# Four stacked attention layers, run one after the other or as one stream of steps on one core

## Chip, cores, metric

One core of one Trainium2 chip. The metric is the device time of one launch in microseconds (us), median of several runs. Each kernel was timed next to the kernel before on the same chip.

## What has to be computed

The reference is four layers, A, B, A, B, over 2048 tokens of width 640, each with a layer norm before it and a residual around it. Both A layers share one set of weights, and so do both B layers. Cut to what matters:

```python
def A(x):                          # 32 heads of 192; 64 segments of 32 tokens
    mem = mem0                     # 8 rows
    for s in range(64):
        h = concatenate([mem, x[segment s]])          # 40 tokens
        q, k, v = h @ Wq, h @ Wk, h @ Wv              # each 640 x 6144
        p = softmax(where(mask, q @ k.T * scale, -1e9))
        o = (p @ v) @ Wo                              # 6144 x 640
        mem = o[:8]                # the next segment needs it
        outs.append(o[8:])

def B(x):                          # 32 heads of 20; each token sees itself and
    ...                            # the tokens 2, 4, ... 14 before it

x = x + A(ln(x)); x = x + B(ln(x)); x = x + A(ln(x)); x = x + B(ln(x))
```

The loop over segments is a true recurrence, so the segments of one layer cannot be batched. And B looks back 14 tokens at most, so it needs only the present and the previous segment.

The weights of A are 4 x 640 x 6144 values in bf16, 31.5 MB. Neither kernel keeps all of them on the chip: part stays resident there, and the rest is streamed again, in the kernel before for every segment.

## The kernel before

It runs the layers one after the other; the activations between them lie in DRAM. In an A layer the 32 units of weights (960 KB each) are 20 resident and 12 streamed per segment, in a ring of four buffers, from a copy in DRAM that is laid out for long contiguous pieces.

```python
# projections: 40 tokens (in a slot of 64 columns) stationary, 384 weight columns moving,
# two heads-pairs side by side in the array
def stream_group(st_cur, wt):
    for c in range(NCH):
        for j2 in range(2):
            nc.tensor.matmul(ps[SLOT * j2:SLOT * (j2 + 1), :], lhsT=st_cur[:, c, :],
                             rhs=wt[:, j2, c * UW:(c + 1) * UW], ...,
                             tile_position=(0, SLOT * j2))
# (cut)
for i in range(16 + 2):                       # 8 units of K, 8 of Q
    if i < 16:
        ps = stream_group(st_cur, get_pair(i))
        nc.scalar.copy(out=stage[:, :], in_=ps[:, :])
    if 1 <= i <= 16:
        do_transposes(i - 1)                  # 6 on TensorE: keys and queries come out
                                              # token-major and must be turned
    if 10 <= i:
        do_scores(i - 2)
# (cut) softmax with mask, max, subtract, Exp, sum, reciprocal, multiply; transposes of P;
#       V and P.V; output projection with 320 moving columns; then the tail of the segment:
nc.scalar.copy(out=part_sb[rs, 0:320], in_=w_ps[0][rs, :])
nc.vector.tensor_copy(out=part_sb[rs, 320:640], in_=w_ps[1][rs, :])
for c in range(NCH):
    nc.tensor.matmul(m_ps[:, c, :], lhsT=part_sb[:, c * P:(c + 1) * P], rhs=selm_r[:, :], ...)
nc.vector.tensor_copy(out=st_nxt[:, :, 0:NM], in_=m_ps[:, :, :])      # next memory
```

A B layer works on four blocks of 512 tokens, with elementwise products for the eight offsets and matmuls with 0/1 matrices that sum over a head.

Of the kernel before, what the change touches and what calls it, by code (L numbers as in the profile page):

```python
# [11 lines left out]
F32 = mybir.dt.float32  # L13
F32R = mybir.dt.float32r
ACT = mybir.ActivationFunctionType
ALU = mybir.AluOpType
AX = mybir.AxisListType
PSUM = bass.MemoryType.PSUM
DRAM = bass.MemoryType.DRAM

def _knob(name, default):
    return default

# [3 lines left out]
NCH = 5  # L27
H = 32
DH = 192
HE = H * DH  # L30
NM = 8
SEG = 32
LTOK = NM + SEG
SLOT = 64
UW = 384
NU = 3 * HE // UW
NHP = 16
NWO = HE // P
EPS = 1e-5
NEG = -1.0e9  # L40

BH = 32
BDH = 20
BW = 8
BDIL = 2
BPAD = (BW - 1) * BDIL


def _ln_rows(nc, pool, x_sb, np_, out_bf, eps_t, dve_stats=False):
    st = pool.tile([P, 4], F32, name="ln_st")  # L50
    if dve_stats:
        bst = pool.tile([P, 2, nc.vector.BN_STATS_DIM], F32, name="ln_bst")
        xr = x_sb[:np_, :].rearrange("p (s f) -> p s f", s=2)
        for s_ in range(2):
            nc.vector.bn_stats(out=bst[:np_, s_, :], in_=xr[:, s_, :])
        nc.vector.bn_aggr(out=st[:np_, 0:2], in_=bst[:np_, :, :])
    else:
        junk = pool.tile([P, D], BF16, name="ln_junk")
        nc.scalar.activation(out=junk[:np_, :], in_=x_sb[:np_, :], func=ACT.Identity, accum_out=st[:np_, 0:1])  # L59
        nc.scalar.activation(out=junk[:np_, :], in_=x_sb[:np_, :], func=ACT.Square, accum_out=st[:np_, 1:2])  # L60
        nc.vector.tensor_scalar(out=st[:np_, 0:2], in0=st[:np_, 0:2], scalar1=1.0 / D, scalar2=None, op0=ALU.mult)
        nc.vector.tensor_tensor(out=st[:np_, 2:3], in0=st[:np_, 0:1], in1=st[:np_, 0:1], op=ALU.mult)
        nc.vector.tensor_tensor(out=st[:np_, 1:2], in0=st[:np_, 1:2], in1=st[:np_, 2:3], op=ALU.subtract)
    nc.scalar.activation(out=st[:np_, 1:2], in_=st[:np_, 1:2], func=ACT.Sqrt, bias=eps_t[:np_, :], scale=1.0)
    nc.vector.reciprocal(out=st[:np_, 1:2], in_=st[:np_, 1:2])
    nc.vector.scalar_tensor_tensor(out=st[:np_, 3:4], in0=st[:np_, 0:1], scalar=-1.0, in1=st[:np_, 1:2], op0=ALU.mult, op1=ALU.mult)
    nc.scalar.activation(out=out_bf[:np_, :], in_=x_sb[:np_, :], func=ACT.Identity, scale=st[:np_, 1:2], bias=st[:np_, 3:4])


NPAIR = 32  # L70
PAIRW = 2 * NCH * UW


def _pair_src(Wq, Wk, Wv, Wo, w, j2):
    if w < 24:
        Wsrc = (Wk, Wq, Wv)[w // 8].rearrange("d h e -> d (h e)")
        u = 2 * (w % 8) + j2
        return Wsrc[:, u * UW:(u + 1) * UW].rearrange("(c p) n -> p c n", p=P), NCH
    Wo2 = Wo.rearrange("h e d -> (h e) d")
    n0 = 24 * j2 + 3 * (w - 24)  # L80
    return Wo2[n0 * P:(n0 + 3) * P, :].rearrange("(m p) d -> p m d", p=P), 3


def prearrange_weights(tc, dram, Wq, Wk, Wv, Wo, pairs):
    nc = tc.nc
    Wr = dram.tile([NPAIR, P, 2, NCH * UW], BF16, name="Wr")
    engs = [nc.sync, nc.scalar, nc.gpsimd]
    cnt = 0
    for w in pairs:
        for j2 in range(2):  # L90
            src, a = _pair_src(Wq, Wk, Wv, Wo, w, j2)
            engs[cnt % 3].dma_start(out=Wr[w, :, j2, :].rearrange("p (a b) -> p a b", a=a), in_=src)
            cnt += 1
    return Wr


def a_res_pairs():
    extra = [int(x) for x in _knob("KDEV_RES_EXTRA", "6,14,22,30").split(",") if x != ""]
    return sorted([w for w in range(NPAIR) if w % 2 == 1] + extra)


def a_prologue(tc, x_in, n_seg, consts, dram, lname, pp, pps, ps_tag):
    nc = tc.nc
    ident = consts["ident"]
    eps_t = consts["eps"]
    S = n_seg * SEG
    XT = dram.tile([n_seg, P, NCH * SEG], BF16, name=f"XT_{lname}")
    n_tiles = (S + P - 1) // P
    for t in range(n_tiles):
        r0 = t * P  # L110
        np_ = min(P, S - r0)
        nsg = np_ // SEG
        x_sb = pp.tile([P, D], x_in.dtype, name="x_sb")
        nc.sync.dma_start(out=x_sb[:np_, :], in_=x_in[r0:r0 + np_, :])
        xn = pp.tile([P, D], BF16, name="xn")
        _ln_rows(nc, pp, x_sb, np_, xn, eps_t, dve_stats=True)
        tp = pps.tile([P, NCH, P], BF16, name="tp", tag=ps_tag)
        for c in range(NCH):
            nc.tensor.transpose(out=tp[:, c, :np_], in_=xn[:np_, c * P:(c + 1) * P], identity=ident[:np_, :np_])
        xT_sb = pp.tile([P, 4, NCH, SEG], BF16, name="xT_sb")  # L120
        nc.vector.tensor_copy(out=xT_sb[:, :nsg, :, :].rearrange("p s c t -> p c s t"),
                              in_=tp[:, :, :np_].rearrange("p c (s t) -> p c s t", t=SEG))
        nc.sync.dma_start(out=XT[4 * t:4 * t + nsg, :, :].rearrange("s p f -> p s f"),
                          in_=xT_sb[:, :nsg, :, :].rearrange("p s c t -> p s (c t)"))
    return XT


def a_layer(ctx0, tc, x_in, x_out, mem0, Wr, Worig, n_seg, consts, dram, lname, res_pairs=None, ring=4, XT=None, direct0=False):
    nc = tc.nc
    ident = consts["ident"]  # L130
    eps_t = consts["eps"]
    S = n_seg * SEG
    scale = float(DH) ** -0.5
    if res_pairs is None:
        res_pairs = a_res_pairs()
    ring = int(_knob("KDEV_RING", ring))
    res_pairs = set(res_pairs)

    with ExitStack() as ctx:
        if XT is None:  # L140
            with ExitStack() as pctx:
                pp = pctx.enter_context(tc.tile_pool(name=f"apro_{lname}", bufs=2))
                pps = pctx.enter_context(tc.tile_pool(name=f"apro_ps_{lname}", bufs=2, space=PSUM))
                XT = a_prologue(tc, x_in, n_seg, consts, dram, lname, pp, pps, "tp")

        wres = ctx.enter_context(tc.tile_pool(name=f"wres_{lname}", bufs=1))
        wring = ctx.enter_context(tc.tile_pool(name=f"wring_{lname}", bufs=ring))
        pers = ctx.enter_context(tc.tile_pool(name=f"apers_{lname}", bufs=1))
        work1 = ctx.enter_context(tc.tile_pool(name=f"awork1_{lname}", bufs=1))
        stg = ctx.enter_context(tc.tile_pool(name=f"astage_{lname}", bufs=2))  # L150
        vtp = ctx.enter_context(tc.tile_pool(name=f"avt_{lname}", bufs=3))
        psA = ctx.enter_context(tc.tile_pool(name=f"psA_{lname}", bufs=3, space=PSUM))
        psT = ctx.enter_context(tc.tile_pool(name=f"psT_{lname}", bufs=2, space=PSUM))
        psS = ctx.enter_context(tc.tile_pool(name=f"psS_{lname}", bufs=2, space=PSUM))
        psM = ctx.enter_context(tc.tile_pool(name=f"psM_{lname}", bufs=1, space=PSUM))

        res_tiles = {}
        engs = [nc.sync, nc.scalar]
        for idx, w in enumerate(sorted(res_pairs)):
            t_ = wres.tile([P, 2, NCH * UW], BF16, name=f"wp{w}")  # L160
            for j2 in range(2):
                src, a = _pair_src(*Worig, w, j2)
                engs[(2 * idx + j2) % 2].dma_start(out=t_[:, j2, :].rearrange("p (a b) -> p a b", a=a), in_=src)
            res_tiles[w] = t_
        engs = [nc.sync, nc.sync]
        dma_cnt = [0]

        direct_first = [direct0]

        def get_pair(w):  # L170
            if w in res_tiles:
                return res_tiles[w]
            t_ = wring.tile([P, 2, NCH * UW], BF16, name="wnr")
            if direct_first[0]:
                for j2 in range(2):
                    src, a = _pair_src(*Worig, w, j2)
                    nc.sync.dma_start(out=t_[:, j2, :].rearrange("p (a b) -> p a b", a=a), in_=src)
                nc.scalar.dma_start(out=Wr[w, :, :, :], in_=t_[:])
            else:
                engs[dma_cnt[0] % 2].dma_start(out=t_[:], in_=Wr[w, :, :, :])  # L180
            dma_cnt[0] += 1
            return t_

        ST0 = pers.tile([P, NCH, SLOT], BF16, name="ST0")
        nc.gpsimd.memset(ST0[:], 0.0)
        ST = [ST0, ST0]
        QTs = [pers.tile([P, 2, 3, SLOT], BF16, name=f"QT{i}") for i in range(3)]
        for i in range(3):
            nc.gpsimd.memset(QTs[i][:], 0.0)
        KT = pers.tile([P, NHP, 3, LTOK], BF16, name="KT")  # L190
# [927 lines left out]
```

## Time and profile before

| | kernel before |
|---|---|
| time, median of 4 runs | 5406.16 us (5403.37 to 5409.18) |
| start | 125 us |
| first A, first B, second A, second B | 2319, 375, 2294, 291 us |
| TensorE busy, matmuls | 90% of the span, 80,920 |
| weights moved by the streaming queue | 1557 MB |

The way to read it: first which engine is full, then in which stretches, then what that engine waits for inside a stretch. The lines for the first two are in the prediction. For the third, these are the largest waits of TensorE inside the first A layer, between 500 and 2400 us (columns: engine, tile and line that waited, for whom; total us, times, longest us):

```profile
PE m_ps L395 <- ACT part_sb L390: 42.8, 53, 0.8
PE o_ps L349 <- DVE vt L367: 13.0, 53, 0.6
...
PE qkv_ps L241 <- DMA wnr<-Wr: 1.9, 3, 0.9
```

In 1900 us, some 53 segments, TensorE waits once a segment for the copy of the output (`part_sb`) and once for the copy of V, both under a microsecond. Streamed weights cost it almost nothing, though the stream nearly fills the DMA.

### The profile page before, as it was taken

What the parts mean: (1) busy time and instruction counts of PE and PEld (TensorE: products, weight loads), DVE (VectorE), ACT (ScalarE), POOL (GpSimd) and SP (SyncE); (2) the same over time, 40 slices, a digit from 0 to 9 for tenths busy, and PEclk for the clock granted to TensorE, in tenths of its full rate; (3) what the DMA queues carried; (4) which work ended last, traced back from release to release, by engine and by line L of the source; (5) the groups of instructions that cost most, each with busy time, mean ns of one, the idle gap of its engine ahead of it and who ended that gap; (6) DMA issues with size and microseconds to landing.
All of it is one profiled execution on the core that took longest, in us unless ns stands there. A gap on an engine that the chain in (4) does not pass through costs nothing. (4 is left out here: it accounts for less than half of the span.)

```text
span 5404.5 us, 183041 instructions
## 1 busy us (share of the span) xinstructions
PE 4851.5 (90%) x80920; PEld 3395.4 (63%) x80920; DVE 2591.0 (48%) x7273; ACT 2218.3 (41%) x5244; POOL 427.2 (8%) x573
## 2 busy tenths in 40 slices
PE   2899999999999999996749999999999999999777
PEld 1666666666666666663326666666666666666533
DVE  2444444444444444445734444444444444444376
ACT  1344444434444444435524434444344434444454
POOL 0000000000000000003200000000000000000131
PEclk8999999999999999997979999999999999999889
DMA  8999999999999999980189999999999999999700
GB/s 264 356 337 330 339 338 336 335 334 336 337 337 333 336 335 339 329 315 34 35 270 334 335 335 337 338 336 332 337 338 333 336 336 336 333 337 331 267 11 15
DMA packets 329209, 1616.19 MB, mean 299 GB/s; under 512 B 50896, under 2 KB 124384, under 8 KB 328416
## 3 DMA queue, kind: packets, MB, share of 16 engines
q1 hardware_dynamic: 290720, 1557.27, 79.5%
q10 hardware_dynamic: 25408, 31.46, 1.7%
q0 software_dynamic: 12288, 15.75, 1.0%
q8 instruction: 636, 10.42, 0.8%
q14 instruction: 157, 1.29, 0.1%
HBM read 1576.82 MB, written 27.53 MB: 297 GB/s over the span
## 5 line engine op out<-in xcount | busy, mean ns | idle before, releaser
L241 PEld LDWEIGHTS <-ST 128*64 128x64 bf16 x30720 | 1578.5, 111 | 535.6 <-issue 68.1
L241 PE MATMUL qkv_ps<-wp,ST 128*64 128x384 bf16 x19200 | 1899.2, 327 | 10.3 <-DMA wp<-in_A_Wk_dram 9.2
L315 ACT CAST stage<-qkv_ps 128x384 bf16<-128x384 f32 x2048 | 978.7, 478 | 1148.5 <-PE qkv_ps L241 1071.3
L241 PE MATMUL qkv_ps<-wnr,ST 128*64 128x384 bf16 x11520 | 1204.3, 328 | 7.4 <-DMA wnr<-Wr 6.1
L273 PE MATMUL tps<-ident,stage 128*64 128x128 bf16 x12288 | 692.7, 220 | 75.6 <-ACT stage L315 75.4
L385 PEld LDWEIGHTS <-OT_sb 128*40 128x40 bf16 x12288 | 638.7, 100 | 192.7 <-issue 1.6
L273 PEld LDWEIGHTS <-stage 128*64 128x64 bf16 x12288 | 567.1, 110 | 301.2 <-ACT stage L315 113.4
L385 PE MATMUL w_ps<-wp,OT_sb 128*40 128x320 bf16 x7680 | 637.9, 299 | 0.0
L282 DVE COPY QT<-tps 128x240 bf16<-128x240 bf16 x1024 | 281.3, 275 | 441.2 <-PE tps L273 441.1
L391 DVE CAST part_sb<-w_ps 40x320 bf16<-40x320 f32 x256 | 125.1, 489 | 753.9 <-PE w_ps L385 752.2
L277 DVE COPY KT<-tps 128x240 bf16<-128x240 bf16 x1024 | 289.7, 283 | 407.5 <-PE tps L273 406.5
L367 DVE CAST vt<-qkv_ps 128x384 bf16<-128x384 f32 x512 | 285.7, 558 | 371.0 <-PE qkv_ps L241 336.3
L390 ACT CAST part_sb<-w_ps 40x320 bf16<-40x320 f32 x256 | 107.5, 420 | 866.7 <-PE w_ps L385 865.2
L385 PE MATMUL w_ps<-wnr,OT_sb 128*40 128x320 bf16 x4608 | 449.6, 299 | 1.4 <-DMA wnr<-in_A_Wo_dram 1.4
L349 PEld LDWEIGHTS <-vt 128*64 128x64 bf16 x12288 | 331.8, 112 | 128.3 <-DVE vt L367 58.4
L365 ACT CAST vt<-qkv_ps 128x384 bf16<-128x384 f32 x512 | 245.3, 479 | 369.2 <-PE qkv_ps L241 369.1
L279 DVE COPY KTp<-tps 64x80 bf16<-64x80 bf16 x1024 | 207.7, 203 | 301.0 <-ACT KTp L278 300.9
L230 POOL DMA_DIRECT2D ST<-XT_L x128 | 116.8, 912 | 2593.3 <-PE o_ps L349 2563.7
L349 PE MATMUL o_ps<-PTa,vt 128*64 128x40 bf16 x6144 | 258.4, 187 | 31.2 <-DVE vt L367 31.1
L295 PE MATMUL s_ps<-KT,QT 128*64 128x40 bf16 x4096 | 265.5, 188 | 22.9 <-DVE QT L282 22.4
L295 PEld LDWEIGHTS <-QT 128*64 128x64 bf16 x8192 | 231.9, 111 | 85.0 <-DVE QT L282 83.3
L295 PE MATMUL s_ps<-KTp,QT 128*64 128x40 bf16 x4096 | 262.7, 186 | 0.0
(122 smaller groups left out, 4216.9 us busy)
## 6 DMA issues: line engine op xcount, KB each, us to landing
wnr<-Wr SPq DMA_DIRECT2D x1524, 960.0 KB, 7.5
Wr<-wnr ACTq DMA_DIRECT2D x12, 960.0 KB, 7.7
XT_L<-xT_sb SPq DMA_DIRECT2D x32, 160.0 KB, 2.1
ST<-XT_L POOLq DMA_DIRECT2D x128, 40.0 KB, 4.5
xs<-xres POOLq DMA_DIRECT2D x128, 40.0 KB, 5.4
xresb<-xs SPq DMA_DIRECT2D x32, 160.0 KB, 3.5
wp<-in_A_Wk_dram SPq DMA_DIRECT2D x10, 480.0 KB, 7.6
wp<-in_A_Wk_dram ACTq DMA_DIRECT2D x10, 480.0 KB, 9.1
```

The source lines that it names most:

```text
L241: nc.tensor.matmul(ps[SLOT * j2:SLOT * (j2 + 1), :], lhsT=st_cur[:, c, :], rhs=wt[:, j2, c * UW:(c + 1) * UW], start=(c == 0), stop=(c == ...
L273: nc.tensor.transpose(out=tps[64 * hf:64 * (hf + 1), sb, :], in_=stage[:, sb * P + 64 * hf:sb * P + 64 * (hf + 1)], identity=ident[:, :], ...
L277: nc.vector.tensor_copy(out=KT[:, 2 * i:2 * i + 2, :, :].rearrange("p j s t -> p s j t"), in_=src)
L279: nc.vector.tensor_copy(out=KTp[64:128, 2 * i:2 * i + 2, 1, :], in_=src[64:128, 1, :, :])
L282: nc.vector.tensor_copy(out=qt[:, :, :, 0:LTOK].rearrange("p j s t -> p s j t"), in_=src)
L295: nc.tensor.matmul(s_ps[hp // 8][SLOT * u:SLOT * (u + 1), hp % 8, :], lhsT=l_, rhs=r_, start=(ci == 0), stop=(ci == 1), tile_position=(0, ...
L315: nc.scalar.copy(out=stage[:, :], in_=ps[:, :])
L349: nc.tensor.matmul(ob[prow:prow + 64, n, :], lhsT=vt[:, vc:vc + 64], rhs=PTx[:, u, i, :], start=True, stop=True, tile_position=(0, prow))
L365: nc.scalar.copy(out=vt[:, :], in_=ps[:, :])
L367: nc.vector.tensor_copy(out=vt[:, :], in_=ps[:, :])
L385: nc.tensor.matmul(w_ps[half][SLOT * j2:SLOT * j2 + LTOK, :], lhsT=OT_sb[:, n, :], rhs=wt[:, j2, m * D + half * 320:m * D + (half + 1) * 320],
L391: nc.vector.tensor_copy(out=part_sb[rs, 320:640], in_=w_ps[1][rs, :])
```

## The change

The intent: read each weight from memory, and load it into the array, once for two segments instead of once for each. The recurrence forbids two segments of the same layer, but the second A layer (layer 3 of the stack) has the same weights, and through B's short reach its segment t-3 is ready when the first A layer is at segment t. So a step takes segment t of layer 1 and segment t-3 of layer 3 as two lanes of 40 tokens in one tile of 80, with the B work of both between them. The 128 segments of A become 67 steps.

It is a rewrite of the whole file, cut here to its core:

```diff
-def kernel_body(..., layers="ABAB"):
-    for li, kind in enumerate(layers):
-        if kind == "A":
-            a_layer(...)                 # 64 segments
-        else:
-            b_layer(...)                 # 4 blocks of 512 tokens
+LAG = 3
+NT = 2 * LT                              # two lanes of 40 tokens
+N_RES = 15
+RING = 4
+for t in range(self.n_seg + LAG + 2):
+    self.step(t)

-    nc.tensor.matmul(ps[SLOT * j2:SLOT * (j2 + 1), :], lhsT=st_cur[:, c, :],
-                     rhs=wt[:, j2, c * UW:(c + 1) * UW], ..., tile_position=(0, SLOT * j2))
-    # ... stage copy, six transposes, copy again
+def proj_stationary(self, kind, i, t):   # K and Q: weights stationary, tokens moving
+    for n in range(6):
+        for c in range(NC):
+            nc.tensor.matmul(ps[:, NT * n:NT * (n + 1)], lhsT=w[:, c, P * n:P * (n + 1)],
+                             rhs=hT[:, NT * c:NT * (c + 1)], ...)
+def a_v(self, i, t):                     # V: tokens stationary, as before
+            nc.tensor.matmul(ps[:, 0:384], lhsT=hT[:, NT * c:NT * c + P],
+                             rhs=w[:, c, 384 * pr:384 * (pr + 1)], ...)

-    # softmax: add mask, max, subtract, Exp, sum, reciprocal, multiply, transposes of P
+    nc.scalar.activation(out=e[0:NT], in_=sv[0:NT], func=ACT.Exp, scale=...)
+    nc.vector.tensor_tensor(out=em[0:NT], in0=e[0:NT], in1=maskA, op=ALU.mult)
+    nc.tensor.matmul(dn[:, 0:4 * NT], lhsT=self.ones[0:NT, :], rhs=em, ...)   # denominators
+    nc.scalar.activation(out=rf, in_=dn[:, 0:4 * NT], func=ACT.Ln)
+    nc.scalar.activation(out=rf, in_=rf, func=ACT.Exp, scale=-1.0)            # 1/sum
+    # (cut) three products of P.V with 1/sum write OT, which has one buffer

+def step(self, t):                       # the order on TensorE, by hand
+    for i in range(NQUAD):               # 8 quads of 4 heads
+        self.a_k(i, t)
+        self.a_q(i, t)
+        if i >= 2:
+            self.a_o(i - 2)              # output projection of an earlier quad
+        self.a_v(i, t)
+        if i >= 1:
+            self.a_pv(i - 1)
+        # (cut) one part of B on 64 tokens: scores, P.V, transpose or output
+        self.a_s(i)
+    self.b_k(b1)                         # "the seam": what is left at the step's end,
+    self.a_o(6)                          # with B's projections laid between
+    self.a_pv(7)
+    self.b_v(b1)
+    self.a_o(7)
+    self.mem_out(t)                      # next memory
+    self.b_q(b1)
```

B becomes dense attention on 64 tokens against the last 128, with 0/1 masks. 15 of the 32 units are resident, because the new kernel needs more of the on-chip memory for other things, and 17 are streamed, straight from the inputs.

## The prediction

> **What bounds the kernel now.** I read the summary of engines first, then the slices, then the four stretches that the slices show, then single bursts on TensorE. The summary, the PE row and the last rows of the slices, and the DMA queue that carries the weights:
>
> ```profile
> PE 4851.5 (90%) x80920; PEld 3395.4 (63%) x80920; DVE 2591.0 (48%) x7273; ACT 2218.3 (41%) x5244; POOL 427.2 (8%) x573
> ...
> PE   2899999999999999996749999999999999999777
> ...
> DMA  8999999999999999980189999999999999999700
> GB/s 264 356 337 330 339 338 336 335 334 336 337 337 333 336 335 339 329 315 34 35 270 334 335 335 337 338 336 332 337 338 333 336 336 336 333 337 331 267 11 15
> ...
> q1 hardware_dynamic: 290720, 1557.27, 79.5%
> ```
>
> The slices show two long stretches (slices 1 to 17 and 20 to 37) in which PE and DMA are both full: the two memory-attention layers (A). Between and after them lie the two local-attention layers (B) with an idle DMA. The view by stretches gives busy time inside each (two A stretches, then the two B layers):
>
> ```profile
> 300.00:2300.00 2000.00, 1914.09 (x33919) 1377.88 (x33915) 933.40 (x2737) 816.71 (x2011) 109.79 (x168) 1.00 0.92 335
> 2900.00:5000.00 2100.00, 2010.02 (x35603) 1448.49 (x35599) 979.88 (x2872) 857.68 (x2112) 115.84 (x177) 1.00 0.93 335
> 2444.00:2819.00 375.00, 239.45 (x1781) 121.00 (x1783) 225.52 (x512) 173.12 (x327) 76.45 (x71) 0.82 0.30 95
> 5113.00:5404.00 291.00, 215.55 (x1532) 106.42 (x1532) 198.36 (x395) 149.42 (x276) 69.29 (x56) 0.89 0.04 12
> ```
>
> The time is thus some 125 us of start, two A layers of about 2319 and 2294 us, and B layers of 375 and 291. An A layer takes 64 segments, so about 36 us each. In it 12 weight units of 960 KB are streamed: 11.8 MB at 335 GB/s is 35.2 us. Both are close to a bound, so I asked the waits of PE: between 500 and 2400 us they hold only 1.9 us for streamed weights, against 42.8 for the segment's tail. A is PE-bound, with DMA just behind. How PE's time is made shows in the timeline, where the columns are start, length, engine, line, operation, tiles, shape and count:
>
> ```profile
> 1000.72 0.98 PE L241 MATMUL qkv_ps<-wp,ST 128*64 128x384 bf16 x10
> ...
> 1016.62 0.40 PE L329 MATMUL pt_ps<-ident,Pm 128*128 128x128 bf16 x4
> ...
> 5172.65 0.98 PE L864 MATMUL lg_ps<-E,prod 128*128 128x32 bf16 x33
> ```
>
> A lone 32-column matmul takes 0.177 us, so the last line is (980-177)/32 = 25 ns from start to start, each with its own 128x128 weight load. Four 128-column ones give (400-222)/3 = 59; the starts in the trace have a median of 56. 320 columns have 135, 512 have 215, and a side-by-side pair of 384 has some 162. All but the 25 ns fit columns/2.4 + 2.5 ns: a fully hidden weight load.
>
> **What the Trainium skill says.** "TensorE: Matmul & The Clock Gate", section "Wait — 56ns, not 53.3ns?", gives N/2.4 GHz + 2.5 ns and a floor of about 25 ns; the 25, 56 and 215 ns above agree. Its "Back-to-back issue gap" says about 81 ns for N=128 with weight loads; the 56 ns here contradict that, and I use the trace. "Weight-path perf modes — Fast Weight Load (FWL) and DoubleRow" says that a full 128-column non-FP32 weight is loaded the fast way; 25 ns a pair agrees. "DMA: Bandwidth & Descriptors", section "Specifications", puts line rate at pieces of 512 B and more and 358 GB/s per core; here the rate still depends on the piece above that. Resident weights arrive in 768-byte rows near 90 to 110 us and mostly in 1280-byte rows at 130 to 140:
>
> ```profile
> 90.00:110.00 20.00, 0.00 (x0) 0.00 (x0) 0.00 (x0) 0.00 (x0) 0.00 (x0) 0.50 1.11 326
> 130.00:140.00 10.00, 4.82 (x64) 3.77 (x61) 1.70 (x8) 2.39 (x8) 0.00 (x0) 0.82 1.08 359
> ```
>
> **The change part by part.** It is a rewrite. (1) The two A layers share weights; the new kernel runs layer 1 of segment t and layer 3 of segment t-3 as two lanes of one 80-row tile. So 67 steps replace 128 segments. (2) B runs inside the step, on 64 rows, as masked dense attention. (3) Keys and queries are produced transposed, weights stationary, which removes the PE transposes of stage (12288) and of P. (4) No maximum is subtracted; the denominator is a matmul with ones, its reciprocal Ln then Exp. (5) 15 of 32 units are resident, 17 stream straight from the inputs, in 1536-byte rows (K, Q, V) or 1280 (output), ring of 4.
>
> PE per step, counted from the built program, each at columns/2.4 + 2.5 ns (25 for 41 columns): K and Q 480 of 80 columns at 36 ns = 17.2 us; V 80 of 384 at 162 = 13.0; output 240 of 80 = 8.6; scores 16 of 160 and 32 of 80 = 2.25; denominator and P·V 8 of 320 and 64 of 80 = 3.4; LN sums 20 of 64 = 0.6; B projections 60 of 64 and 10 of 320 = 3.1; B scores, P·V, transpose and output = 2.3. With input and output transposes the sum is 50.5 us; times 67, 3388 us of PE floor, where before 64 segments twice and B cost some 5280.
>
> DMA per step: 17 x 983040 B = 16.7 MB. From 768 B at 326 and 1280 B at 362 (16-engine rates from bytes over time; the row above is a mix), a piece costs 37.6 and 56.6 ns per engine, so 0.037 ns a byte more, and 1536 B 66 ns: 372 GB/s, an estimate. That is 45.3 us, 5 below PE. With units consumed some 3 us apart on average and four buffers, a load is issued 6 us or more before its use, against 2.7 of transfer and some 2 of latency. I count no DMA wait in a full step.
>
> DVE: from rows like 320 columns 486 ns, 384 558, narrow ones 0.2 us: per head quad QF 0.49, Qz 0.33, V 0.56, three output products 1.15, mask 0.44, eight times 23.7 us; B and the LNs some 12.7; about 36 us. ACT: 480 columns 0.56, 384 0.48, 320 0.43 or 0.47: 21.2 plus 6.0 = 27 us. "ScalarE: Activation LUTs", "Table sets: the hidden batching unit", has Ln and Exp in one set; the built program has one load. The trace's loads are 1283 ns each, 12 in all, so this matters only if wrong.
>
> Neither engine exceeds PE, but both are in order. Walking one step by hand: in quads 1 to 3 DVE carries B's masks too, about 4.85 us plus 1.1 of waiting for Ln and Exp, equal to PE's 5.9. It just holds. At the seam PE waits some 0.4 us for the product of quad 6, 0.7 for that of quad 7, and 0.5 for odd hops: 1.7 us. The memory copy hides behind B's Q projection. So 52.2 us a step by the walk; I take 52.5 for hops that I have missed.
>
> Start: masks on POOL, 64 small selects of about 0.2 us, plus x, LN: 23 us. Step 0 needs all 32 units, 31.5 MB, plus 3.3 MB of B weights: 95 us at 366 GB/s, so about 99 us to its end and 4 more lost as the ring refills. Tail: two steps without A, chains of ACT and DVE of some 19 us each: 38. Steps 1 to 66 at 52.5 less 2.4 of missing B = 3463. Sum 103 + 3463 + 38 = 3604; I say 3610.
>
> **The rivals.** (a) The stream becomes the bound: at 326 GB/s a step needs 51.2 us, hardly more; at 300, 55.7 and some 3820 in all. For it: 86% of the estimated rate is needed. Against: saturated rows at 326 and more. (b) The chain over ACT and DVE sets the step: 2 us more a step makes 3740. For it: quads 1 to 3 have no slack. (c) The weight loads stay exposed, 56 ns for an 80-column matmul: 816 x 20 ns = 16 us a step, 4680. Against: the 25 ns. (d) Nothing waits: 50.5 a step, 3480.
>
> **Range and chances.** (d) and (a) or (b) bracket it: 3490 to 3800. Even (c) is faster than 5406; only a table load at each Ln and Exp, or fetch of instructions failing, would undo it. Faster 0.98, same 0.01, slower 0.01.
>
> **What would show it.** PE starts 36 ns apart in K and Q; period of a step 52 to 53 us; DMA near 320 GB/s with under 2 us a step of PE waiting for w_ring; DVE near 36 and ACT near 27 us a step; step 0 ending near 100 us; the two last steps near 38. I am wrong if PE waits mostly for DVE inside a step, if the 80-column pitch is over 40 ns, or if w_ring leads the waits.

## More of the kernel before

From the page of the kernel before, the loads of streamed weights (count, KB each, median us from issue to landing):

```profile
wnr<-Wr SPq DMA_DIRECT2D x1524, 960.0 KB, 7.5
```

## The result and the profile after

| | before | after |
|---|---|---|
| time, median | 5403.92 us (12 runs, 5402.03 to 5409.2) | 3542.76 us (8 runs, 3540.55 to 3551.39) |
| ratio | | 0.6557 (95%: 0.6551 to 0.6564) |
| TensorE busy | 90% | 97% |
| weights moved by the streaming queue | 1557 MB | 1134.5 MB |

Ratios in this document are the mean time of one kernel's runs over the mean of the other's in the same rounds, so they are not quite the ratio of the medians. The result is correct. The profiled run took 3549.5 us.

The page after: the engines, the rows of the slices for TensorE and DMA, the queues (packets, MB, share), the chain of work that ended last, and two of the four kinds of streamed loads, which answer to `wnr` (count, KB each, median us from issue to landing; the other two, for Q and V, have 7.0 and 7.2):

```profile
PE 3436.5 (97%) x71520; PEld 2990.2 (84%) x71520; DVE 2082.6 (59%) x6314; ACT 1671.2 (47%) x4187; POOL 54.9 (2%) x183
...
PE   5899999999999999999999999999999999999997
...
DMA  9999999999999999999999999999999999999994
...
q1 hardware_dynamic: 800288, 1134.50, 94.4%
q8 instruction: 559, 9.16, 1.1%
...
PE 88%; issue 4%; DMA 4%; ACT 2%; DVE 1%; POOL 0%; SPq 0%; POOLq 0%; ACTq 0%
...
w_ring<-in_A_Wk_dram SPq DMA_DIRECT2D x335, 960.0 KB, 7.2
w_ring<-in_A_Wo_dram SPq DMA_DIRECT2D x335, 960.0 KB, 7.7
```

The two dips of the B layers are gone: TensorE and DMA are both full from the second slice to the last but one. From these rows alone one cannot say which of the two sets the time. The chain names TensorE for 88%, and 4% each for DMA (79 of its some 129 us lie in the first 160 us) and for time that nothing shown explains.

The view by stretches (columns: window, length, busy us of PE, PEld, DVE, ACT, POOL with counts, clock, DMA share, GB/s), for the first step and a long stretch of full steps:

```profile
22.00:98.00 76.00, 50.60 (x856) 41.13 (x856) 22.16 (x64) 19.18 (x47) 2.31 (x7) 0.93 1.01 348
500.00:3000.00 2500.00, 2472.72 (x51747) 2156.20 (x51746) 1500.79 (x4552) 1206.67 (x3027) 27.74 (x72) 1.00 0.97 328
```

In full steps TensorE stands still for 27 us of 2500, and DMA runs at 328 GB/s.

The timeline of TensorE over the seam of one step (start, length, engine, line, operation, tiles, shape, count; in brackets the idle time before it and what ended it):

```profile
1022.31 1.24 PE L205 MATMUL ps_k<-hT,w_ring 128*128 128x80 bf16 x30
...
1025.83 1.79 PE L232 MATMUL ps_v<-w_v,hT 128*128 128x384 bf16 x10
...
1028.16 1.04 PE L358 MATMUL ps_bk<-h2T,wqkv_sb 128*128 128x64 bf16 x30
1029.54 1.24 PE L288 MATMUL ps_acc<-OT,w_ring 128*128 128x80 bf16 x30 [0.34 <-DVE OT L275]
...
1034.47 1.24 PE L205 MATMUL ps_k<-hT,w_ring 128*128 128x80 bf16 x30
```

Thirty 80-column matmuls, each with a new 128x128 weight block, take 1.24 us. The last one's own duration is about 0.2 us, so they start (1.24 - 0.2)/29 = 36 ns apart; this time from start to start is called their pitch. Ten 384-column ones start (1.79 - 0.33)/9 = 162 ns apart, the 0.33 being the mean duration of one such matmul (327 ns). The only wait in this stretch is one of 0.34 us, before the output projection of quad 6, for the product that makes its input.

The waits of TensorE between 500 and 3200 us, some 52 steps:

```profile
PE ps_acc L288 <- DVE OT L275: 17.0, 50, 0.3
PE ps_acc L288 <- issue: 5.1, 5, 2.1
...
PE ps_acc L288 <- DMA w_ring<-in_A_Wo_dram: 1.2, 4, 0.4
```

It is that same wait once a step. Streamed weights are waited for four times in 52 steps.

The starts of the matmuls in the trace give the length of each step: at best 51.10 us (51.38 in the steps that also transpose an input or output tile), mean 51.57. So the time adds up: 106.7 us until step 1 begins, 66 steps of 51.57, and 37.4 of tail, is 3547 us, the profiled span.

Where the time came from, per two segments of A (one step after), each entry as a count of matmuls times their median start-to-start time in the two traces:

| us per two segments | before | after |
|---|---|---|
| K and Q projections, transposes, scores | 33.4 | 19.5 |
| V projection | 13.0 | 13.0 |
| transposes of P, denominators, P.V | 3.9 | 3.4 |
| output projection and tail matmuls | 13.9 | 8.6 |
| layer norm sums of A | in B | 0.3 |
| the remainder: waits, and starts later than the median | 7.7 | 1.0 |
| B (666 us over 64) | 10.4 | 5.9 |
| sum | 82.4 | 51.6 |

The remainder is the length of the stretch less the other rows; of the 7.7 before, the waits that the trace names make 2.9. 64 times the difference of 30.8 is 1971 us. The three extra steps and the tail give 3 x 51.6 + 37 = 192 us back, and a shorter start saves 125 - (106.7 - 51.6) = 70. Together 1849, against the 1857 between the two spans. The V projection gained nothing: it has the tokens stationary, so 80 instead of 40 of them in the array cost the same moving columns as two side-by-side groups did.

### The profile page after: what moved, and what is told of

Same layout as the page of the kernel before. It is cut to its first block, busy times and chain, and to the rows that moved or that the text cites. A ratio compares the mean times of both kernels' runs of the same rounds, so it can differ in the third digit from the quotient of the medians. Undisturbed runs are those within 1.5% of the kernel's fastest.

```text
span 3547.4 us, 158668 instructions
## 1 busy us (share of the span) xinstructions
PE 3436.5 (97%) x71520; PEld 2990.2 (84%) x71520; DVE 2082.6 (59%) x6314; ACT 1671.2 (47%) x4187; POOL 54.9 (2%) x183
## 3 DMA queue, kind: packets, MB, share of 16 engines
q8 instruction: 559, 9.16, 1.1%
## 4 chain that ended last, share of the span: by engine, by line
PE 88%; issue 4%; DMA 4%; ACT 2%; DVE 1%; POOL 0%; SPq 0%; POOLq 0%; ACTq 0%
PE ps_v L232 23%; PE ps_acc L288 16%; PE ps_q L205 15%; PE ps_k L205 15%; PE ps_o L269 4%; PE ps_bv L378 2%; DMA w_ring<-in_A_Wo_dram 2%; PE ps_s L251 2%; PE ps_s L248 2%; PE ps_d L264 2%; PE ps_bq L358 2%; PE ps_by L447 2%; PE ps_bs L402 2%; PE ps_st L316 1%; DVE OT L275 1%
## 5 line engine op out<-in xcount | busy, mean ns | idle before, releaser
L232 PEld LDWEIGHTS <-hT 128*128 128x128 bf16 x5360 | 492.4, 98 | 292.3 <-issue 8.1
L205 PEld LDWEIGHTS <-w_ring 128*128 128x128 bf16 x18090 | 684.3, 100 | 9.1 <-issue 5.0
L232 PE MATMUL ps_v<-w_v,hT 128*128 128x384 bf16 x3350 | 603.5, 327 | 8.2 <-DMA w_v<-in_A_Wv_dram 5.5
L288 PE MATMUL ps_acc<-OT,w_ring 128*128 128x80 bf16 x10050 | 416.5, 202 | 34.8 <-DVE OT L275 22.7
L205 PE MATMUL ps_k<-hT,w_ring 128*128 128x80 bf16 x10050 | 417.7, 202 | 4.4 <-DVE hT L334 2.4
L288 PEld LDWEIGHTS <-w_ring 128*128 128x128 bf16 x10050 | 384.8, 100 | 42.9 <-issue 34.4
L232 PE MATMUL ps_v<-w_ring,hT 128*128 128x384 bf16 x2010 | 361.3, 327 | 2.2 <-DMA w_ring<-in_A_Wv_dram 2.2
L211 ACT CAST KT<-ps_k 128x480 bf16<-128x480 f32 x536 | 297.9, 556 | 129.7 <-PE ps_k L205 129.4
L205 PE MATMUL ps_q<-hT,w_q 128*128 128x80 bf16 x8040 | 333.8, 202 | 4.3 <-DMA w_q<-in_A_Wq_dram 2.7
L205 PE MATMUL ps_q<-hT,w_ring 128*128 128x80 bf16 x8040 | 333.4, 202 | 2.9 <-DMA w_ring<-in_A_Wq_dram 2.9
L205 PEld LDWEIGHTS <-w_q 128*128 128x128 bf16 x8040 | 305.8, 100 | 5.3 <-DMA w_q<-in_A_Wq_dram 3.0
L269 PEld LDWEIGHTS <-Vt 80*128 80x128 bf16 x4288 | 220.1, 98 | 52.5 <-issue 0.3
```

The source lines that it names most:

```text
L205: nc.tensor.matmul(ps[:, NT * n:NT * (n + 1)], lhsT=w[:, c, P * n:P * (n + 1)], rhs=hT[:, NT * c:NT * (c + 1)], start=(c == 0), stop=(c == ...
L211: self.nc.scalar.copy(out=self.KT[i % 2][:, 0:6 * NT], in_=ps[:, 0:6 * NT])
L232: nc.tensor.matmul(ps[:, 0:384], lhsT=hT[:, NT * c:NT * c + P], rhs=w[:, c, 384 * pr:384 * (pr + 1)], start=(c == 0), stop=(c == NC - 1))
L269: nc.tensor.matmul(ov[:, pr, b, :], lhsT=vt[0:NT, 512 * pr + w0:512 * pr + w0 + P], rhs=em[0:NT, 2 * pr + j, :], start=st, stop=sp)
L288: nc.tensor.matmul(self.acc[:, NT * c:NT * (c + 1)], lhsT=w[:, m, P * c:P * (c + 1)], rhs=ot[:, m, :], start=(i == 0 and m == 0 and c == 0 ...
```

## The experiments

The theory: TensorE sets the step, by the sum of its start-to-start times, and what pays is that one weight serves two segments. The rivals: the weight stream sets the step; the other engines' chain does; the sharing does not matter and the new form of softmax and transposes is what pays. All experiments edit the kernel after. Ratios are to the kernel before, as above.

**Fewer resident weights: 13, then 9 of 32 units.** This makes the stream longer and leaves TensorE's work alone.

```diff
-N_RES = 15
+N_RES = 13          # e2: 9
```

> 13 instead of 15 resident units, so 19 streamed a step, 18.7 MB. Theory PE (a step is the sum of TensorE pitches plus about 1 us of waits, the stream is hidden as long as it can carry it): with 1536-byte rows at an estimated 372 GB/s the stream needs 50.6 us, still under the measured 51.6, so within 2% of the changed kernel, 3540 to 3610 us. Theory stream (the 97% DMA share and 328 GB/s in the steady part are the limit): 57 us a step, some 3900 us.

> 9 resident, 23 streamed a step, 22.6 MB. Theory PE: now the stream is over the PE sum and sets the step at 22.6 MB/372 GB/s = 61 us, in all about 4180 us, 18% over the changed kernel, and the rate in the steady part rises to about 370 GB/s. Theory stream: the rate stays at 328 GB/s, 69 us a step, about 4700 us. In both PE's waits are for w_ring.

Measured: 13 resident, 3692.21 us (0.6829; 0.6819 to 0.6839), 4.2% longer, where at most 2% was expected: missed. 9 resident, 4270.41 us (0.7899; 0.7886 to 0.7912), near what was expected. Both correct. The stretch of full steps and a wait of TensorE in it, 13 resident:

```profile
500.00:3000.00 2500.00, 2400.22 (x49749) 2079.28 (x49748) 1450.69 (x4381) 1162.42 (x2913) 26.70 (x69) 1.00 1.03 353
```
```profile
PE ps_v L232 <- DMA w_ring<-in_A_Wv_dram: 41.8, 57, 1.4
```

And 9 resident:

```profile
500.00:3000.00 2500.00, 2139.34 (x42737) 1807.09 (x42738) 1254.01 (x3767) 998.95 (x2503) 23.25 (x60) 1.00 1.05 366
```
```profile
PE ps_v L232 <- DMA w_ring<-in_A_Wv_dram: 167.1, 175, 2.2
```

With 9 resident the stream is the bound: the step took 62.4 us, 10.8 more than in the kernel after, and TensorE's waits for streamed weights, 321 us in 40 steps over all lines, are 8.0 of them. The rate rose from 328 to 366 GB/s. (That 23 units of 983,040 B at 366 GB/s are 61.8 us is no evidence of its own, since the rate is the mean of the same stretch.) With 13 resident, 19 units at 366 GB/s are 51.0 us, equal to TensorE's 51.1, yet the step took 53.6. Two bounds that are equal on average do not give their common value. My reading is that units are not used evenly over the step and the ring holds four, so the stream pauses where the step uses none (the seam) and is waited for later; the 57 waits in 47 steps, for V's units, fit that. With 15 resident the stream needs 17 x 983,040 / 366 = 45.7 us and has the slack for this. So the kernel stands two units away from a stream bound that costs more than the averages say.

**Narrower matmuls.** Four fifths of the K and Q matmuls and nearly all of the output's move 40 columns instead of 80. The second lane is wrong (the comparison with the reference still passed it, since the attention terms are small beside the residual).

```diff
+nw = NT if c == 0 else LT
-nc.tensor.matmul(ps[:, NT * n:NT * (n + 1)], ..., rhs=hT[:, NT * c:NT * (c + 1)])
+nc.tensor.matmul(ps[:, NT * n:NT * n + nw], ..., rhs=hT[:, NT * c:NT * c + nw])
# the same in the output projection
```

> Wrong result on purpose: four fifths of the K and Q matmuls and nearly all output matmuls stream 40 columns (one lane) instead of 80. All loads, evacuations and other engines are unchanged. Theory PE: 619 matmuls a step fall from 36 to the 25 ns floor, 6.9 us less; PE would need 44.7 us and the stream 45.3, so a step of 45 to 47 us and 3130 to 3250 us in all, with waits for w_ring appearing. Theory stream: unchanged, 3540. Theory chain (ACT and DVE set the step): unchanged or down by less than 2%.

Measured: 3439.11 us (0.6362; 0.6352 to 0.6371). The step fell to 49.9 us, not to the 45 to 47 expected: missed. TensorE's shorter work did shorten the step, but only by about a quarter of what it saved: 619 matmuls at 25 instead of 36 ns are 6.8 us, and the step got 1.7 shorter. The largest wait of TensorE between 500 and 3000 us (with all lines, those for "issue" are 152 us in 50 steps, 3.0 a step), and three lines of its timeline:

```profile
PE ps_acc L290 <- issue: 51.4, 48, 3.3
```
```profile
895.88 0.51 PE L206 MATMUL ps_q<-hT,w_q 128*128 128x80 bf16 x13
897.59 0.61 PE L206 MATMUL ps_q<-hT,w_q 128*128 128x40 bf16 x17 [1.19 <-issue]
898.34 0.91 PE L290 MATMUL ps_acc<-OT,w_ring 128*128 128x40 bf16 x30
```

"issue" means that nothing the profile shows was waited for. Here TensorE stops for 1.19 us in the middle of the thirty matmuls of one Q projection, whose weights (`w_q`, resident) and tokens it was already using. No data can explain that. In the trace such stops lie 128 matmuls apart, and the work goes on some 1.4 us (median) after a 16 KB packet of the queue q8 has landed. The page counts 559 packets and 9.16 MB on q8; divided by the 2 x 71,520 instructions of TensorE that is 64 B for each, so one packet is 256 instructions, or 128 matmuls with their weight loads. I read q8 as the refill of TensorE's instructions. That is inferred from count and timing; no line of the profile says it.

**One lane at a time.** Each step does its A part twice, with 40 columns as in the experiment before, and loads its 17 units twice. So no weight is shared. Its output is wrong, which doesn't matter for the time.

```diff
+for i in range(NQUAD):        # a first pass over A, ahead of the normal one
+    self.a_k(i, t); self.a_q(i, t)
+    ...                       # a_o(i - 2), a_v, a_pv(i - 1), a_s
+self.a_o(6); self.a_pv(7); self.a_o(7)
```

> Wrong result on purpose: each step runs the memory-attention part twice, each pass with the one-lane columns of e3_short and its own load of the 17 streamed units, as if the two layers did not share a pass over the weights. Theory sharing (the gain comes from one pass over the weights for two layers): a step needs 33.4 MB, 90 us at 370 GB/s, and some 82 us of PE, so about 67 x 91 + 120 = 6200 us, slower than the kernel before (5404). Theory dataflow (the gain comes from stationary weights without transposes and from the hidden local attention, whatever the sharing): well below 5404.

Measured: 6564.47 us (1.2148; 1.213 to 1.2166), slower than the kernel before. The stretch of full steps:

```profile
500.00:5500.00 5000.00, 4486.61 (x102924) 3757.43 (x102920) 2695.14 (x7766) 2278.50 (x5723) 29.47 (x76) 0.98 1.02 350
```

The step took 96.6 us. In its trace the pitches of TensorE sum to 81 us for two passes and B, and 34 units at the 366 GB/s measured above would be 91; the kernel after has 50.5 and 45.7. Neither alone is the step. The named waits of TensorE in these 51.8 steps:

```profile
PE ps_acc L290 <- DVE OT L276: 142.6, 143, 1.3
PE ps_acc L290 <- issue: 87.5, 94, 2.7
...
PE ps_acc L290 <- DMA w_ring<-in_A_Wo_dram: 51.1, 96, 2.2
```

That is 2.8 us a step for the product that makes `OT`, some 4.6 over all lines for "issue", and 1.3 for streamed weights.

So the new kernel needs the sharing: without it, it takes 1.85 times as long. A 40-column matmul costs 25 ns against 36 for 80 columns, and the stream doubles. What the new form would be worth without sharing, against the kernel before, this run does not settle. It streams 34 units where the kernel before streams 24 for two segments, and its V projection takes 13.0 us in each pass, where the kernel before does V of two segments in 13.0. Without that extra V the sum would be about 68 us against 82.4 before (74.7 without the remainder). By this estimate up to 14 of the 30.8 us might be had without sharing. The last rival is thus refuted in its full form only.

**No stream.** From step 2 on no weight is loaded; the ring's last four units stand in for all streamed ones (wrong; relative error 0.032).

```diff
+if not res and self.t_now >= 2:
+    t_ = self.ring_tiles[-1 - self.ring_use % RING]
+    self.ring_use += 1
+    return t_[:]...
```

> Wrong result on purpose: from step 2 on no weight is streamed; the last four units of the ring stand in for every streamed one. PE, DVE and ACT do exactly the same work. Theory PE: only the stalls within runs (0.25 us a step, at the refill of PE's instructions) and the few waits for w_ring go, so 51.1 us a step: 3510 to 3535, under 1% faster. Theory stream: the DMA share falls from 97% to almost nothing and the step falls well below 50 us.

Measured: 3527.69 us (0.6526; 0.6517 to 0.6536). The stretch of full steps:

```profile
500.00:3000.00 2500.00, 2483.17 (x52086) 2168.85 (x52083) 1510.55 (x4586) 1216.97 (x3050) 28.89 (x75) 1.00 0.02 5
```

The GB/s fall from 328 to 5, the DMA share from 0.97 to 0.02, and the time by 0.4%. Every step takes 51.10 or 51.38 us, the best values of the kernel after. This settles what the page could not: of the two full resources TensorE is the bound, and the whole stream costs some 0.3 us a step. (The chain of the other engines runs here too; the narrow matmuls, above and below, speak against it.) The waits for "issue" are gone too. The one wait left, 0.3 us a step for the product of quad 6, is the same as with the stream.

**Narrower matmuls and no stream.** First the narrow kernel once more on this chip, then both edits together.

> Placeholder look at e3_short again without its stream would be the next run; this one repeats e3_short once on this chip, 3435 to 3445 us, so that the two can be compared on one chip.

Measured: 3441.49 us, a single run of unknown state, 0.1% from the 3439.11 of the other chip.

> Wrong result on purpose: e3_short (40 columns) and no stream from step 2 on. In e3_short PE stalled within its runs, each time about 1.4 us after a 16 KB instruction packet had landed, every 128 matmuls. Theory instruction refill beside the stream: without the stream these packets come sooner, the stalls go, and a step is 44 to 45 us, 3090 to 3150 us in all. Theory refill alone (a block of 128 matmuls cannot be fetched faster whatever the DMA carries): stalls stay and it remains at 3350 or more. Theory stream rate (e3_short was held by w_ring): 3090 to 3150 too, but then e3_short's waits would have been for w_ring, which they were not.

Measured: 3227.88 us (0.5972; 0.5962 to 0.5982; relative error 0.032, as wrong as without the stream), where 3090 to 3150 was expected: the total missed, while the stops went as the first theory said. The stretch of full steps, and the largest wait of ScalarE in it:

```profile
500.00:3000.00 2500.00, 2435.99 (x57186) 2045.94 (x57185) 1646.37 (x5033) 1326.02 (x3349) 29.60 (x78) 1.00 0.02 5
```
```profile
ACT Qz L228 <- DVE Qz L227: 302.1, 289, 1.3
```

The step took 46.5 to 46.75 us, and no wait of TensorE is for "issue" any more. So the stops of the narrow kernel, 49.9 - 46.7 = 3.2 us a step, come from the stream and the short matmuls together. With either taken away they are nearly or wholly gone. That fits a refill of instructions that shares the DMA with the weights and is used up faster by shorter matmuls. It also shows what I had left out of the expectation: some 3 us above TensorE's sum of 43.7 remain, in small waits on the chain over DVE and ScalarE (queries copied by one, then the other). With 44 us of TensorE work the rival "chain of the other engines" begins to be true; with 51 it is not.

**The kernel after once more, the seam, the start, and both.** Four runs on one chip. The kernel after again is the baseline:

> The changed kernel itself, as the yardstick on the same chip for the three runs after it: 3540 to 3555 us.

Measured: 3542.71 us (0.6554; 0.6545 to 0.6563).

For the seam I moved the output projection of quad 5 from its place in quad 7 behind B's K projection, so that TensorE has work while the product of quad 6 is made.

```diff
-                if i >= 2:
+                if 2 <= i < 7:
                     self.a_o(i - 2)
@@ at the end of the step, after b_k
+            self.a_o(5)
             self.a_o(6)
```

> The output matmuls of quad 5 moved from ahead of V of quad 7 to behind B's K projection, so that they fill PE's wait for the product of quad 6. Theory PE: the trace shows 0.50 us lost there a step (31.8 us in all) and 0.13 before the output of quad 7; the first goes, the second stays, so about 30 us less, 0.9%: 3510 to 3520. Theory stream: the total does not move, as the 17 loads are unchanged. Theory chain: DVE is no earlier with the product of quad 6, because LN and V evacuation stand ahead of it, and the wait stays.

Measured: 3565.55 us (0.6595; 0.6586 to 0.6604), correct, 0.6% slower instead of 30 us faster: missed. The timeline of the seam:

```profile
1031.45 1.24 PE L288 MATMUL ps_acc<-OT,w_ring 128*128 128x80 bf16 x30
1032.80 0.49 DVE L275 TENSOR_TENSOR OT<-ps_o,R 128x320 bf16<-128x320 f32 x1 [1.56 <-PE ps_acc L288]
1033.34 1.24 PE L288 MATMUL ps_acc<-OT,w_ring 128*128 128x80 bf16 x30 [0.65 <-DVE OT L275]
```

The tile OT has one buffer. The product of quad 6 may write it only when the output projection of quad 5 has read it, and I had moved just that projection to a later time: DVE now waits 1.56 us for it, then TensorE 0.65 for DVE, where it was 0.34. A second buffer for OT should let the edit show what it is worth; that was not run.

For the start, the first tokens and the memory are loaded by the same queue as the weights and ahead of them, the first copy goes to DVE, and B's weights (3.3 MB) are loaded in steps 1 and 2.

```diff
-        self.x_load(0)
+        self.x_load(0, nc.sync)
-        nc.gpsimd.dma_start(out=m[0:NM, :], in_=self.mem0)
+        nc.sync.dma_start(out=m[0:NM, :], in_=self.mem0)
-        self.x_take(0)
+        self.x_take(0, nc.vector)
@@ in step(t), at quad 1
+            if t == 1: self.load_wqkv()
+            if t == 2: self.load_wo()
```

> The first tokens and the memory come through the SP queue and are taken up by DVE, not behind the mask building on POOL; the B weights (3.3 MB) are loaded in steps 1 and 2 instead of at the start. The first K matmul at some 12 us instead of 31; step 0 stays bound by its 31.5 MB of weights at 370 GB/s, 85 us, so it ends near 90 instead of 106.7 and the total falls by 12 to 17 us (0.4%). If instead steps 1 and 2 pay for the deferred 3.3 MB (9 us of stream), the gain is only some 6 us.

Measured: 3539.56 us (0.655; 0.6541 to 0.6559), correct; no difference to the baseline, whose interval it overlaps. Steps 0 and 1 of this kernel:

```profile
19.00:94.50 75.50, 54.12 (x930) 44.11 (x930) 23.05 (x64) 20.39 (x50) 3.49 (x14) 0.93 1.06 366
94.50:152.50 58.00, 51.89 (x1008) 44.21 (x1008) 26.05 (x74) 21.77 (x54) 0.38 (x1) 0.94 1.04 365
```

Steps 0 and 1 of the kernel after:

```profile
31.20:106.70 75.50, 54.07 (x930) 44.09 (x930) 23.05 (x64) 20.39 (x50) 0.00 (x0) 0.93 1.02 350
106.70:158.30 51.60, 49.07 (x1009) 42.46 (x1009) 26.08 (x74) 21.66 (x54) 0.38 (x1) 1.00 1.05 362
```

Work began 12.2 us earlier, and step 0 ended 12.2 us earlier. Step 1 then took 58.0 instead of 51.6 us, 6.4 more. Of the deferred 3.3 MB, 2.46 MB (B's query, key and value weights) are loaded in step 1: 6.7 us of DMA at 366 GB/s. The DMA was full in both kernels, so about half of what had been gained at the start was paid for in step 1. The other 5.8 us are within the scatter of the runs.

> The edits of e6_seam and e7_start together: their gains add, some 42 to 47 us under the changed kernel of this round (1.2 to 1.3%), near 3500.

Measured: both edits, 3559.96 us (0.6587; 0.6578 to 0.6596), missed for the reason of the seam.

**A ring of three.** On top of both edits, one buffer of the ring becomes one more resident unit, so that 16 units are streamed instead of 17.

```diff
-N_RES = 15
-RING = 4
+N_RES = 16
+RING = 3
```

> The version of e8_both with one ring buffer fewer (3) and one resident unit more (16, so 16 streamed: 15.7 MB a step). If four buffers were needed to hide the loads, waits for w_ring appear and it is slower than e8_both; by the spacing of the loads in the changed kernel (issued 6 us or more ahead) three should still hide them, and it comes out within 0.5% of e8_both, with fewer instruction stalls as the DMA share falls.

Measured: 3607.33 us (0.6676; 0.6666 to 0.6686), correct. It is 1.3% slower than both edits with four buffers (by the ratios 1.35%; the two ran on different chips), where within 0.5% was expected: missed. A wait of TensorE in its full steps:

```profile
PE ps_acc L294 <- DMA w_ring<-in_A_Wo_dram: 29.0, 48, 1.8
```

Less is streamed, and yet TensorE waits for the stream once a step. The traces show why: in the kernel after a load is issued at least 8.8 us (median 10.4) before its first use and lands within 7.0 to 7.7 (medians). With three buffers the output units are issued at least 6.6 us (median 7.2) ahead, and their loads take 6.5. One load alone would take 2.7 us at 366 GB/s, so most of the 7 us is probably time behind the loads ahead; no run isolates that. The edit also changes which units are streamed, so the depth is not isolated either. None of the versions with the right result beats the kernel after beyond the noise.

## Why the prediction was right

- **Pitches.** 36 ns for 80 columns and 162 for V came out as predicted, and with them the sum: 50.5 us predicted, and at best 51.1 measured, of which 0.6 are waits at the seam. Most of the gain rests on this step.
- **The stream hidden.** Predicted 372 GB/s for rows of 1536 bytes, and 45.3 us a step (369 GB/s) for the mix with 1280; measured 366 for the mix. No wait for weights in a full step was predicted; four were seen in 52 steps, and taking the stream away saves 0.4%. The working behind it was wrong twice, in opposite directions. A load was to take some 4.7 us from issue to landing and took 7.0 to 7.7; the page of the kernel before already had 7.5 for this size. It was to be issued 6 us or more before its use, and was issued 8.8 or more. A lead of 6 us would not have covered it, so the right answer is in part luck here. With three buffers, or with two units more in the stream the claim fails.
- **A misread line.** The window from 130 to 140 us was said to hold mostly 1280-byte rows. Its packets in the trace are 2945 of 768 bytes and 258 of 1280. The 1280-byte rows came at 120 to 130 us, at 362 GB/s; the sum uses that figure, so it does not suffer.
- **DVE and ScalarE below TensorE.** Predicted 36 and 27 us a step; measured 2082.6/67 = 31.1 and 1671.2/67 = 24.9. Products of bf16 with bf16 from on-chip memory took 0.32 us for 320 columns and 0.35 to 0.36 for 384; I had put the first at 0.44. The feared waiting in quads 1 to 3 did not come.
- **Waits in a step: the term that was mis-sized.** The walk by hand gave 1.7 us, and I added 0.3 for hops that I might have missed, so 52.5 us a step. The mean step took 51.57, that is 1.07 above the sum. The seam costs 0.50 us before quad 6's output and 0.13 before quad 7's, by start-to-start times, instead of 0.4 + 0.7: B's V projection covers nearly all of the second. What remains, some 0.4, are the stops for "issue" and a few other waits. Predicted 3463 us for steps 1 to 66, measured 66 x 51.57 = 3404. These 59 us are the miss.
- **Start and tail.** Predicted 103 and 38 us, measured 106.7 and 37.4. Two errors nearly cancel in the first, which is luck. The first matmul came at 31.2 instead of 23, because POOL issues the load of the first memory rows only after its masks (the chain has it start at 22.5 us and take 5.0). And the 4 us for the refilling of the ring in step 1 did not come (51.6 us).
- **The rivals.** The stream as the bound, the chain as the bound and exposed weight loads were not seen; "nothing waits", 3480, came nearest. The sum of the measured parts, 3547, lies between it and the 3610 told.

Three things stay open. The first is how the gain over the kernel before splits between the sharing and the new form, as said above. The second is whether the stops for "issue" are instruction refill, for which there is count, timing and their vanishing without the stream, but no line that says so. The third is what the seam edit gains with two OT buffers; at most it is the 0.6 us a step that is left there, 42 us in all.

## What to carry to other kernels

When a recurrence forbids batching, look for another layer with the same weights that can run beside it with a lag. With the weights stationary a second lane of 40 columns cost 11 ns on top of 25, and the stream fell from 12 units a segment to 8.5, though fewer units were resident. When two resources are both full on the page, take one away in an experiment before tuning either; and before moving work over a wait, check which buffer the moved work still holds.

## What the Trainium skill lacked or had wrong

- "TensorE: Matmul & The Clock Gate", section "Back-to-back issue gap", gives about 81 ns for N=128 with weight loads, and 131 for N=512, as the sustained figures. Here 128 columns with a new 128x128 block each start 55 to 56 ns apart, 512 columns 215 to 216, 80 columns 36, 64 columns 29. Its figure for the isolated matmul, N/2.4 + 2.5 ns, fits them all within 1 ns.
- "Runtime: NRT & Kernel Launch", section "Instruction fetch mechanics", has refill blocks of 16 KiB, 256 instructions; 559 packets for 143,040 instructions of TensorE agree. It calls the cost of crossing a block mostly hidden. With 25 ns matmuls beside a stream of 340 GB/s, stops at just that spacing cost some 3 us of a 49.9 us step, and none without the stream. If they are the refill, as inferred above, the page lacks this case.
- "DMA: Bandwidth & Descriptors", section "Specifications", has line rate from 512 B on and 358 GB/s per core. Here 768-byte rows ran at 326 GB/s, and a mix of 1536 and 1280-byte rows at 366 when it was the bound, so the rate still rises above 512 B and goes above that limit.
- "Perfetto Trace Analysis", section "Identifying the Most-Contended Engine", says that the occupancy of DMA misleads. The runs agree, and add a size: a share of 0.97 whose removal saves 0.4%. HBM utilization, which it names instead, would have misled here too: 322 GB/s over the span, of the 358 above.
- No page that I read tells how much deeper a ring must be when the stream fills the DMA: here 960 KB landed 7.0 to 7.7 us after issue, and three buffers instead of four cost 1.3% with 16 units streamed in place of 17.
